# The order in which an instruction's waits are listed, in a gated mix of full and sliding-window attention

## The chip, the cores and the metric

The kernel runs on one core of one Trainium2 chip. The metric is the device time of one execution in microseconds (us). The median of three runs of the kernel before is 833.99 us, the lowest 832.91 and the highest 834.21.

## What is computed

Two attention blocks read the same input `x` (2048 tokens, width 640, 32 heads of 20) and are mixed by a gate per token.

```python
def _A_ref(x, wqkv, wo):                 # full attention
    q, k, v = qkv[0], qkv[1], qkv[2]
    scores = jnp.einsum("bhqd,bhkd->bhqk", q, k) * scale
    p = _softmax(scores, axis=-1)
    o = jnp.einsum("bhqk,bhkd->bhqd", p, v)
    return o.transpose(...).reshape(B, S, D) @ wo
def _B_ref(x, wqkv, wo):                 # 8 keys, each 2 apart, looking back
    idx = pos[:, None] - (jnp.arange(8) * 2)[None, :]
    logits = jnp.einsum("bhsd,bhswd->bhsw", q, kg) * scale
    attn = _softmax(jnp.where(mask, logits, -1e9), axis=-1)
    ...
g = _sigmoid((x * gate_w).sum(-1, keepdims=True))
return g * a + (1 - g) * b
```

## The kernel before

**Full attention.** The work is cut into 32 groups: 4 blocks of 512 queries by 8 quads of heads (four heads lie on the four 32-row strips of TensorE). A group has 64 units, one for each of 16 key blocks and 4 heads: a matmul of keys by queries into one PSUM bank of 512 columns. Two or three units make a tile. For each tile s, `qk(s)` (L1524) writes the scores to `score[s % 2]`, and `exp(s)` (L1547) on ACT turns them into `ebuf[s % 5]`. `pv` (L1592) multiplies the exps by the values and accumulates them in `obank`. So tile s+2 can't be scored before exp(s) has read its buffer, and exp(s) writes a buffer that exp(s-5) wrote and that pv has read since.

Some units take another way ("rides"): a third matmul of `qk` goes into a side bank, and DVE makes an exponential out of it by integer arithmetic on bf16 bits (L1537 into `uD`, L806 with shifted copies into `eD`), for which GpSimd scales the values (L798 into `vS`).

**Everything else** is fitted in between: projections, the gate, the sliding attention B (L841 to L1000), the normalisation of each group (L767 to L781) and the output projection. Their matmuls go through `mm_group` (L566) into three side banks, two of which are the third banks of the score buffers. L1613 is a filler matmul.

**What sets the order.** A planner, `_Sched`, is run while the program is built. `task()` lays out each operation on one of five streams (SP for DMA issues, ACT, PE, DVE, POOL), finds the earlier tasks that it must wait for (`deps`: for each stream the youngest task alone, its own included, and each DMA for itself), and estimates its `end` from given durations and from the delay `LAT` of each stream (0.22 us for PE, 0.18 ACT, 0.13 DVE, 0.15 POOL, 0.1 SP). `idx` is a task's number in the order of layout. `next_tile`, `step`, `spend` and the generators use these estimates to choose what is laid out next.

`emit()` then writes each stream out in its order. For each task it goes through the task's `deps` and calls `wait_ge` for each semaphore value that this stream hasn't waited for yet; then it issues the operation. In the built program an instruction holds one wait: the first wait listed for a task stays on its (first) instruction, and each further one becomes an instruction of its own ahead of it, EVENT_SEMAPHORE in the profile, all of them from L285. For an exp of the kernel before, the list is the wait for exp(s-5) on ACT's own semaphore and then the wait for `qk(s)` on PE's. The first sits on the exp; the second is the separate instruction ahead of it. A DMA's wait for its own semaphore's earlier use follows after these.

By engine, the built program of before has this many instructions with two or more waits, and separate wait instructions in all:

| | instructions | with several waits | separate waits |
|---|---|---|---|
| ACT | 764 | 742 | 751 |
| PE | 12389 | 423 | 447 |
| DVE | 1191 | 164 | 166 |
| POOL | 194 | 25 | 29 |
| SP | 723 | 118 | 131 |

Of the kernel before, what the change touches and what calls it, by code (L numbers as in the profile page):

```python
# [115 lines left out]
LAT = {"pe": 0.22, "act": 0.18, "dve": 0.13, "pool": 0.15, "sp": 0.1}  # L116
# [20 lines left out]
class _Sched:  # L137
# [107 lines left out]
    def emit(self):  # L245
        for sname in self.STREAMS:
            ccount = 0
            pool = self.dma_sems.get(sname)
            rot = 0
            totals = {}  # L250
            for t in self.lists[sname]:
                if not t.mark:
                    continue
                if t.dom == "cmp":
                    ccount += 1
                    t.sem = self.sems[sname]
                    t.val = ccount
                else:
                    sem = pool[rot % len(pool)]
                    rot += 1  # L260
                    prev = totals.get(sem, 0)
                    t.sem = sem
                    t.prev_total = prev
                    t.val = prev + 16 * t.nd
                    totals[sem] = t.val
            for sem, tot in totals.items():
                self.dma_final[sem] = tot
        nc = self.nc
        names = {"sp": "sync", "act": "scalar", "pe": "tensor", "dve": "vector", "pool": "gpsimd"}
        with nc.allow_low_precision(reason="bf16 kernel"), nc.allow_non_contiguous_dma(  # L270
            reason="small layout loads"
        ), nc.Block() as blk:
            for sname in self.STREAMS:
                lst = self.lists[sname]
                if not lst:
                    continue

                def body(eng, lst=lst, sname=sname):
                    waited = {}
                    for t in lst:  # L280
                        for d in sorted(t.deps, key=lambda x: x.idx):
                            if d.val is None:
                                raise RuntimeError("unmarked dep")
                            if d.val > waited.get(d.sem, 0):
                                eng.wait_ge(d.sem, d.val)  # L285
                                waited[d.sem] = d.val
                        if t.dom == "dma" and t.prev_total > waited.get(t.sem, 0):
                            eng.wait_ge(t.sem, t.prev_total)
                            waited[t.sem] = t.prev_total
                        ins = t.fn(eng)  # L290
                        if t.mark:
                            group = ins if isinstance(ins, list) else [ins]
                            assert len(group) == t.nd and group[0] is not None
                            for i_ in group:
                                i_.then_inc(t.sem, 16 if t.dom == "dma" else 1)
                    if sname == "sp":
                        for sem, tot in self.dma_final.items():
                            if tot > waited.get(sem, 0):
                                eng.wait_ge(sem, tot)

                getattr(blk, names[sname])(body)
# [1485 lines left out]
```

## Time and profile before

| | |
|---|---|
| median of the runs | 833.99 us (832.91 to 834.21) |
| span of the profiled execution, first to last instruction | 830.2 us |
| granted TensorE clock over the span | 0.999 |
| first and last start of an exp (L1547) | 19.1 and 818.3 us |
| HBM read, written | 11.94 MB, 2.62 MB |
| DMA queue of the loads and copies, share of 16 engines | 12.5% |

The profile is of one execution. Its span leaves out what lies before the first and after the last of the program's own instructions, 3.8 us against the median of the runs. Busy times on PE come from modelled ends of pipelined matmuls; on ACT and DVE one instruction's record overlaps the next one's, so the pace is read from starts. Semaphore instructions aren't counted as busy. A wait is credited to the engine that met it last.

### The profile page before, as it was taken

What the parts mean: (1) busy time and instruction counts of PE and PEld (TensorE: products, weight loads), DVE (VectorE), ACT (ScalarE), POOL (GpSimd) and SP (SyncE); (2) the same over time, 40 slices, a digit from 0 to 9 for tenths busy, and PEclk for the clock granted to TensorE, in tenths of its full rate; (3) what the DMA queues carried; (4) which work ended last, traced back from release to release, by engine and by line L of the source; (5) the groups of instructions that cost most, each with busy time, mean ns of one, the idle gap of its engine ahead of it and who ended that gap; (6) DMA issues with size and microseconds to landing.
All of it is one profiled execution on the core that took longest, in us unless ns stands there. A gap on an engine that the chain in (4) does not pass through costs nothing.

```text
span 830.2 us, 29189 instructions
## 1 busy us (share of the span) xinstructions
PE 776.4 (94%) x12389; PEld 284.4 (34%) x12389; DVE 679.5 (82%) x1191; ACT 802.8 (97%) x763; POOL 139.1 (17%) x194
## 2 busy tenths in 40 slices
PE   8999999998999899999999998899999999998898
PEld 5332232333333332333244233333333433343223
DVE  7667787789989878887898988898887977889973
ACT  4999999999999999999999999999999999999995
POOL 5022111620211111021201011111011111101110
PEclk9999999999999999999999999999999999999999
DMA  9112210200111010011001011100111011100001
GB/s 310 35 36 47 47 35 19 71 21 15 36 34 31 24 29 20 7 40 34 18 18 44 19 20 41 31 22 7 34 30 27 6 39 33 33 7 21 21 6 34
DMA packets 45014, 29.12 MB, mean 35 GB/s; under 512 B 27204, under 2 KB 43684, under 8 KB 44884
## 3 DMA queue, kind: packets, MB, share of 16 engines
q1 hardware_dynamic: 44596, 26.92, 12.5%
q8 instruction: 98, 1.61, 0.8%
q10 hardware_dynamic: 288, 0.33, 0.1%
q14 instruction: 32, 0.26, 0.1%
HBM read 11.94 MB, written 2.62 MB: 18 GB/s over the span
## 4 chain that ended last, share of the span: by engine, by line
ACT 49%; PE 34%; issue 13%; DVE 4%; DVEq 0%; ACTq 0%
ACT ebuf L1547 49%; PE score L1524 10%; PE obank L1592 8%; PE side L566 8%; PE score L566 4%; DVE uD L1537 1%; DVE eD L806 1%; PE obank L468 1%; PE score L1239 1%; PE obank L1613 1%; ACT eB L923 0%; PE side L1262 0%; PE score L1613 0%; ACT tB L957 0%; PE score L693 0%
## 5 line engine op out<-in xcount | busy, mean ns | idle before, releaser
L1547 ACT ACTIVATE ebuf<-score 128x1024 bf16<-128x1024 f32 (+1 forms) x731 | 791.4, 1232 | 8.8 <-PE score L1524 6.7
L1524 PE MATMUL score<-qT,kT 32*128 32x512 bf16 x2048 | 290.9, 383 | 35.9 <-ACT ebuf L1547 24.3
L1537 DVE TENSOR_SCALAR uD<-score 128x512 int16<-128x512 f32 x324 | 217.1, 684 | 41.6 <-PE score L1524 38.9
L806 DVE TENSOR_SCALAR eD<-uD 128x2048 int16<-128x2048 int16 x243 | 169.0, 725 | 5.8 <-PE obank L1592 5.2
L1524 PEld LDWEIGHTS score<-qT,kT 32*128 32x128 bf16 x2048 | 74.9, 91 | 281.7 <-ACT ebuf L1547 121.0
L1592 PE MATMUL obank<-ebuf,vA 128*21 128x512 bf16 x1724 | 160.3, 385 | 2.6 <-ACT ebuf L1547 1.9
L798 POOL TENSOR_TENSOR vS<-vA,vw 128x252 bf16<-128x252 bf16 x81 | 60.2, 744 | 317.0 <-PE obank L1592 283.7
L566 PE MATMUL side<-xT,kvw 128*32 128x256 bf16 (+1 forms) x2540 | 102.6, 280 | 2.1 <-DVE qkvB L862 1.0
L1592 PE MATMUL obank<-eD,vS 128*21 128x512 bf16 x972 | 83.4, 379 | 0.3 <-DVE eD L806 0.3
L566 PEld LDWEIGHTS side<-xT,kvw 128*32 128x32 bf16 x2540 | 59.6, 96 | 34.8 <-issue 19.0
L1592 PEld LDWEIGHTS obank<-ebuf,vA 128*21 128x21 bf16 x1724 | 38.0, 89 | 87.7 <-issue 74.6
L773 POOL TENSOR_TENSOR rcp<-rcp,gA 128x16 f32<-128x16 f32 x31 | 8.7, 282 | 280.2 <-DVE rcp L771 280.2
L979 DVE TENSOR_TENSOR stage<-qkvB,repB 128x1280 bf16<-128x1280 bf16 x64 | 52.9, 852 | 0.0
L878 DVE TENSOR_TENSOR stage<-qkvB 128x1280 bf16<-128x1280 bf16 x64 | 52.6, 850 | 0.2
L862 DVE CAST qkvB<-side 128x512 bf16<-128x512 f32 (+1 forms) x72 | 42.0, 593 | 9.3 <-PE side L566 9.0
L566 PE MATMUL side<-stage,ident 128*32 128x512 bf16 (+1 forms) x736 | 47.9, 349 | 1.7 <-DVE oB L996 0.9
L779 POOL TENSOR_TENSOR oN<-oTt,rcp 128x512 bf16<-128x512 f32 x31 | 32.9, 1062 | 2.4
L767 DVE STREAM_TRANSPOSE oTt<-obank 128x512 f32<-128x512 f32 x32 | 22.8, 712 | 11.2 <-PE obank L1592 10.7
L1592 PE MATMUL obank<-uD,vA 128*21 128x512 bf16 x324 | 31.5, 379 | 0.0
L1592 PEld LDWEIGHTS obank<-eD,vS 128*21 128x21 bf16 x972 | 23.5, 91 | 16.2 <-issue 2.5
L1613 PE MATMUL obank<-xT,zero 128*32 128x512 bf16 x296 | 26.6, 384 | 0.0
L566 PE MATMUL side<-woA_d,oTd 128*32 128x512 bf16 (+2 forms) x520 | 26.0, 295 | 0.0
(169 smaller groups left out, 542.0 us busy)
## 6 DMA issues: line engine op xcount, KB each, us to landing
repB<-eB SPq DMA_DIRECT2D x128, 32.0 KB
WqP<-in_A_wqkv_dram SPq DMA_DIRECT2D x16, 160.0 KB
stage<-in_B_wqkv_dram SPq DMA_DIRECT2D x1, 2400.0 KB
oTd<-oN SPq DMA_DIRECT2D x108, 20.0 KB
qT<-dst SPq DMA_DIRECT2D x104, 20.0 KB
out_dram<-outsb SPq DMA_DIRECT2D x12, 160.0 KB
kvw<-in_A_wqkv_dram SPq DMA_DIRECT2D x2, 800.0 KB
oTd<-in_A_x_dram SPq DMA_DIRECT2D x2, 640.0 KB
```

The lines of the kernel that those rows point to most:

```text
L566: ins = e.matmul(o[j:k, :], l(j) if callable(l) else l[:, j:k], r, start=(first and i == 0), stop=(last and i == n - 1), skip_group_check= ...
L779: T(en, c2, lambda e: e.tensor_tensor(oo, ii, ib, ALU.mult), reads=["rcp", "oTt"], writes=["oN0"])
L798: T("pool", 0.7, lambda e: e.tensor_tensor(vS[:, d % 2, :, :], _ap(vA, (kb * NQ + q) * 4 * DV, [[0, K - 1], [1, 4 * DV]]), _ap(vw, 0, [[1, ...
L806: T("dve", 0.11 + 0.1334 * n, lambda e, k=k, sl=sl: e.tensor_scalar(eD[:, sl % NS, 0:512 * n].bitcast(I16), uD[d % 2][:, 0:512 * n].bitcas ...
L862: t = TB(dvc(n * TOK), lambda e, o=o, i=i: e.tensor_copy(o, i), reads=[("side", b)], writes=[key])
L878: TB(dvc(CN * TOK, 2), lambda e, w=w, ks=ks: e.tensor_tensor(prodB(w), qB[:, :, :], ks, ALU.mult), reads=["qB", "kB"], writes=[("prod", w) ...
L979: TB(dvc(CN * TOK, 2), lambda e, w=w, vs=vs, rr=rr: e.tensor_tensor(prodB(w), vs, rr, ALU.mult), reads=["vB", ("repB", w4 % NR)], writes=[ ...
L1524: ins = e.matmul(o, kT[32 * j:32 * j + 32, q, kb * P:(kb + 1) * P], qT[g % NQT][32 * j:32 * j + 32, :], start=True, stop=True)
L1537: t = T("dve", 0.69, lambda e: e.tensor_scalar(uD[d % 2][:, 512 * i:512 * (i + 1)].bitcast(I16), side[x], UOFF, 0.0, op0=ALU.add, op1=ALU. ...
L1547: exps[s] = T("act", actc(512 * n), lambda e: e.activation(ebuf[s % NE][:, 0:512 * n], score[s % 2][:, 0:512 * n], ACTF.Exp, scale=LN2 / S ...
L1592: ins = e.matmul(obank[32 * j:32 * j + DV, :], v, src, start=(kb == 0), stop=(last and k >= len(lst) - 4), skip_group_check=True)
L1613: ins = e.matmul(o[32 * j:32 * j + 32, :], w[:, 32 * j:32 * j + 32] if best else w[:, :], xT[:, 0, 0:512], start=bool(best), stop=bool(bes ...
```

## The change

The waits of a task are sorted by the time at which the planner expects each to be met, `end` plus the delay of its stream, the latest first. Before, they were sorted by `idx`, the oldest in the layout first.

```diff
                     for t in lst:
-                        for d in sorted(t.deps, key=lambda x: x.idx):
+                        for d in sorted(t.deps, key=lambda x: -x.end - LAT[x.stream]):
                             if d.val is None:
                                 raise RuntimeError("unmarked dep")
                             if d.val > waited.get(d.sem, 0):
```

The plan itself, what runs on which engine and in which order, isn't touched. The sorted list decides which wait sits on the instruction and which ones stand apart, ahead of it. For an exp the list becomes `qk(s)` on PE's semaphore and then exp(s-5), so the wait for the scores sits on the exp. Where a stream waits twice for one semaphore, the larger value may now come first and make the smaller one unnecessary: PE has 446 separate waits after, and the other engines' numbers are the same.

## Prediction

> **What bounds the kernel now.** I read the page first: the busy line, the chain, the largest groups.
>
> ```profile
> span 830.2 us, 29189 instructions
> PE 776.4 (94%) x12389; PEld 284.4 (34%) x12389; DVE 679.5 (82%) x1191; ACT 802.8 (97%) x763; POOL 139.1 (17%) x194
> ...
> ACT 49%; PE 34%; issue 13%; DVE 4%; DVEq 0%; ACTq 0%
> ...
> L1547 ACT ACTIVATE ebuf<-score 128x1024 bf16<-128x1024 f32 (+1 forms) x731 | 791.4, 1232 | 8.8 <-PE score L1524 6.7
> ```
>
> ACT and PE share the bound, and 13% of the chain is "issue", in which nothing the profile names was running. The 8.8 us of idle time before the exps is too kind: consecutive ACT records overlap. By their start times, an exp of 1024 columns follows another after 904 ns at best and one of 1536 after 1330 ns. 469 of the one and 262 of the other make 469 x 0.904 + 262 x 1.330 = 772 us. The exps run from 19.1 to 819.3 us, so some 28 us in this stretch are not exp at full pace. In 144 places the next start came straight off a wait; these lost 18.4 us against that spacing.
>
> Next, the waits view, and the view of line 285, where every separate wait instruction comes from.
>
> ```profile
> PEld score L1524 <- ACT ebuf L1547: 121.0, 288, 1.2
> ...
> DVE uD L1537 <- PE score L1524: 38.9, 72, 2.0
> ```
>
> ```profile
> L285 ACTq EVENT_SEMAPHORE  x749: 17/17/38, 10.5 to 826.1; - x188
> L285 PEldq EVENT_SEMAPHORE  x445: 51/51/1052, 4.0 to 823.1; - x149
> L285 DVEq EVENT_SEMAPHORE  x164: 21/21/907, 17.7 to 825.3; - x164
> L285 POOLq EVENT_SEMAPHORE  x25: 17/17/17, 4.3 to 784.4; - x25
> ```
>
> PE and ACT hand work back and forth; almost every exp, and 445 places on PE, pass through a separate wait. Such a record takes 17 to 51 ns, but what a handover costs is not its length. So I took, for each instruction that waits, the time at which its last semaphore reached the awaited count (the trace's semaphore records, joined with each engine's waits in program order) and its start. Where the engine was free, the delays fall into two sharp groups:
>
> ```
> last wait met is on:     the instruction itself   a separate wait ahead of it
> ACT  release to start          22 ns                   82 ns
> DVE  release to start          23 ns                   92 ns
> POOL release to start          67 ns                  132 ns
> PE   to weight load            41 ns                  104 ns
> PE   to first matmul           45 ns                  135 ns
> PE   to end of 3-matmul scores 461 ns                 548 ns
> ```
>
> The timeline shows the last kind directly:
>
> ```profile
> 740.46 0.10 PEld L1524 LDWEIGHTS score<-qT,kT 32*128 32x128 bf16 x3 [0.21 <-ACT ebuf L1547]
> 740.46 0.39 PE L1524 MATMUL score<-qT,kT 32*128 32x512 bf16 x3
> ...
> 741.24 0.13 PEld L1524 LDWEIGHTS score<-qT,kT 32*128 32x128 bf16 x3 [0.36 <-issue]
> 741.27 0.39 PE L1524 MATMUL score<-qT,kT 32*128 32x512 bf16 x3 [0.20 <-ACT ebuf L1547]
> ```
>
> The first group has one wait, and load and matmul start together; the second has two, and the matmul starts 0.03 us behind its load, as if the instructions behind the separate wait were fetched only once it had ended.
>
> **The change, part by part.** It adds and removes no work: every engine has the same instructions in the same order, and the number of separate waits stays (751 on ACT, 166 on DVE, 29 on POOL, 131 on SP; 447 becomes 446 on PE). What moves is which wait sits on the instruction: it differs in 742 instructions of ACT, 331 of PE, 160 of DVE, 24 of POOL and 47 DMA issues of SP. The first wait listed stays on the instruction. By layout that is the oldest task: for an exp, its own engine's exp five tiles back, met microseconds ago, so the wait for the scores, which ends last, stands apart. The new list puts the scores' wait on the exp.
>
> Price of one handover, from the rows above: ACT 82 - 22 = 60 ns; PE 548 - 461 = 87 ns; DVE 92 - 23 = 69 ns, say 70; POOL 65 ns.
>
> How many are on the path? I followed the trace back from the last instruction: to the releaser where a start lay at one of the delays above, else to the instruction before it on its engine. (The page's chain can't be used for this count: a separate wait may end while ACT still runs the exp before, and the chain hops to PE all the same.) The path has 221 handovers and no DMA. Last met on a separate wait before and on the instruction after, by the release times of this trace: 74 on ACT, 49 on PE, 18 on DVE. Nine more on PE keep their late wait apart, 71 have it on the instruction in both.
>
> Sum along this path: 74 x 0.060 + 49 x 0.087 + 18 x 0.070 = 4.4 + 4.3 + 1.3 = 10.0 us. More than that can't go as long as durations stay, since this path remains.
>
> It may be less, for another path may take over. The lower reading cuts each handover to what its engine stood still beyond its usual spacing (904 or 1330 ns on ACT; 205 to 315 ns on PE by the pair of lines): 3.5 on ACT, 3.5 on PE, 1.3 on DVE, together 8.3 us. The paths that take over have separate waits too, so they shorten as well; but some run long on ACT alone. I take 8.3, and 10.0 as the far end.
>
> What is taken at nothing:
> - A separate wait that is met early. On PE, a score group behind an out-projection group starts after 312 ns with or without one; 162 of 215 exps whose scores had been ready over 320 ns start at full pace to 5 ns. Their number stays, so if this cover failed it would cost the same before and after.
> - Waits that the new order puts wrongly: by this trace 7 on PE and 2 on POOL go from the instruction to a separate wait, but only two of them bind: 2 x 0.087 = 0.2 us if both came onto the path; they are not on it now.
> - SP's 47 DMA issues. No row prices them; by the other engines' rows each may come 0 to 70 ns earlier. Nothing on the path waits for a DMA, so 0.
> - POOL, 22 such handovers at 65 ns, with 691 us idle and none on the path: 0.
>
> The stall removed goes to the other waits of the same loop: PE's single waits for ACT (148 starts, 35 us of excess spacing) are on the instruction already and don't shrink.
>
> 830.2 - 8.3 = 821.9 us of span. The runs' median is 834.0, 3.8 us over the span; with this kept, 825.7.
>
> [...]
>
> **The rivals.**
> 1. *The gain is taken back by another bound.* If PE's and DVE's part only lengthens waits elsewhere, ACT's handovers cut to lost spacing remain: 3.5 us, 830.5 us. For it: PE is 94% busy and ACT 97%; 23 of the 74 ACT handovers have less than 50 ns of lost spacing. Against: ACT lost 18.4 us behind PE and PE 78 us in excess spacing, both far more than the gain.
> 2. *The delay belongs to having several waits, not to which one is last.* Then 834.0. Against: of PE's starts with several waits, those 12 whose last one was on the instruction and bound came at 41 ns like single ones. For: it is only these few, and none on ACT.
> 3. *Slower: DVE and GpSimd collide more.* Starts move by up to 10 us, and the 243 shifted-copy operations of DVE take 906 ns on average where GpSimd is at work beside them (45 of them) and 684 ns elsewhere.
>
> ```profile
> L806 DVE TENSOR_SCALAR eD<-uD x243: 629/686/1798, 49.3 to 807.7; 128x2048 int16<-128x2048 int16 x122
> ```
>
> Each new collision costs 0.22 us if the path waits for it. 38 more eat the 8.3 us; 90 in place of 45 would give 825.7 + 10.0 = 835.7, if all were on the path. For it: the spread to 1798 ns. Against: GpSimd is busy 17% and follows the same order; this line has 12.3 us of the path in all, at some 0.7 us each 17 of the 243.
>
> **How the numbers follow.** The forecast, a gain of 5 to 11 us, has 0.82; rival 1, 0.11; rival 2, 0.04; rival 3, 0.03. Time 825.7. The range runs from 823.0 (the 10.0 us, with 1 us for the runs' own spread of 832.9 to 834.2) to 829.5 (half of PE's and DVE's part lost as in rival 1, 834.0 - 3.5 - 2.4 = 828.1, and the same spread). A measurement of this kernel can tell about 0.2%, 1.7 us, from no change: faster is the forecast and nearly all of rival 1, 0.93; same 0.04; slower 0.03.
>
> **What would show it.** In the profile after: exps bound by the scores start 22 ns behind the release; score matmuls start with their weight load, not 0.03 us behind; PE's groups end 461 ns behind the release; ACT's 18.4 us of lost spacing shrink to 9 to 12; the share of "issue" in the chain falls. The prediction is wrong if the delays move as said and the span doesn't (rival 1), if delays with late waits attached stay at 82 and 104 (rival 2), or if the 906 ns class of line 806 grows (rival 3).

## The result, and the profile after

| | kernel before | kernel after |
|---|---|---|
| median of the first five runs each | 833.99 us | 827.38 us (827.07 to 827.95) |
| ratio, 95% interval | | 0.9928 [0.9916, 0.9940] |
| measured again, other executions of before | 831.83 us median of 15 (831.70 to 834.04) | 827.94 us (827.01 to 829.45), ratio 0.9949 [0.9936, 0.9962] |
| span of the profiled execution | 830.2 us | 826.0 us |

The kernel is faster, by some 0.5 to 0.7%. The two ratios differ because the kernel before varies from one execution to the next, between 831.7 and 834.3 us; its first five runs happened to lie high. By these ratios the gain is 4.2 to 6.0 us; from profile to profile it is 4.2 us.

The page after, the same lines:

```profile
span 826.0 us, 29186 instructions
PE 775.0 (94%) x12387; PEld 281.2 (34%) x12389; DVE 679.2 (82%) x1191; ACT 800.2 (97%) x763; POOL 140.7 (17%) x194
...
ACT 52%; PE 25%; issue 20%; DVE 3%; ACTq 0%; DVEq 0%
...
L1547 ACT ACTIVATE ebuf<-score 128x1024 bf16<-128x1024 f32 (+1 forms) x731 | 789.3, 1275 | 6.7 <-PE score L1524 5.7
```

The busy times are those of before (two matmul records fewer were kept and one separate wait is less, no work is gone). "issue" has grown from 13 to 20%, though waits became shorter; the prediction had it fall. The share says little of the time: in a run shown below, which leaves out nearly all separate waits of ACT and has the same span of 826.0 us, it is 0%:

```profile
ACT 75%; PE 22%; DVE 2%; issue 0%; DVEq 0%
```

The chain goes by whichever wait the profile ties to an instruction, and the change moves just these. The line to look at is the exp's: its mean record grew from 1232 to 1275 ns, with the same shapes. That is the subject of most of what follows.

The waits view, the view of line 285 and the shifted copies:

```profile
PEld score L1524 <- ACT ebuf L1547: 202.9, 483, 1.2
...
DVE uD L1537 <- PE score L1524: 38.4, 69, 2.1
```

```profile
L285 ACTq EVENT_SEMAPHORE  x749: 17/17/38, 10.0 to 821.9; - x188
L285 PEldq EVENT_SEMAPHORE  x444: 51/51/842, 4.0 to 819.0; - x148
L285 DVEq EVENT_SEMAPHORE  x164: 21/21/564, 16.8 to 819.0; - x164
L285 POOLq EVENT_SEMAPHORE  x25: 17/17/17, 4.3 to 776.3; - x25
```

```profile
L806 DVE TENSOR_SCALAR eD<-uD x243: 628/683/1805, 49.6 to 803.7; 128x2048 int16<-128x2048 int16 x122
```

As many separate waits as before, as short as before: their records alone don't show the change. The 121.0 us that PE's loads waited for ACT became 202.9, but 88.0 us of "issue" at the same place became 45.6, and the idle time before these loads is 281.7 us in one page and 282.0 in the other: again a matter of who is named. DVE's shifted copies are unchanged.

In the timeline, the group that stood for the slow handover before:

```profile
737.52 0.10 PEld L1524 LDWEIGHTS score<-qT,kT 32*128 32x128 bf16 x3 [0.30 <-ACT ebuf L1547]
737.52 0.39 PE L1524 MATMUL score<-qT,kT 32*128 32x512 bf16 x3
...
738.50 0.13 PEld L1524 LDWEIGHTS score<-qT,kT 32*128 32x128 bf16 x3 [0.54 <-DVE uD L1537]
738.53 0.39 PE L1524 MATMUL score<-qT,kT 32*128 32x512 bf16 x3
```

At 737.52 load and matmul now start together. At 738.50 they don't: this is a group whose last wait still stands apart. The delays from release to start, taken as in the prediction, are ACT 22 ns (113 starts), DVE 23, POOL 68, PE 41 to the load, 45 to the matmul and 461 to the end of the group; on the 32 starts of PE that still wait apart 104, 135 and 548.

### The profile page after: what moved, and what is told of

It is laid out like the page before. It is cut to its first block, busy times and chain, and to the rows that moved or that the text cites. A ratio compares the mean times of both kernels' runs of the same rounds, so it can differ in the third digit from the quotient of the medians.

```text
span 826.0 us, 29186 instructions
## 1 busy us (share of the span) xinstructions
PE 775.0 (94%) x12387; PEld 281.2 (34%) x12389; DVE 679.2 (82%) x1191; ACT 800.2 (97%) x763; POOL 140.7 (17%) x194
## 4 chain that ended last, share of the span: by engine, by line
ACT 52%; PE 25%; issue 20%; DVE 3%; ACTq 0%; DVEq 0%
ACT ebuf L1547 51%; PE score L1524 8%; PE obank L1592 5%; PE side L566 5%; PE score L566 4%; DVE uD L1537 1%; PE score L1239 1%; PE obank L468 1%; DVE eD L806 1%; ACT eB L923 0%; PE obank L1613 0%; PE side L1262 0%; ACT tB L957 0%; PE score L1613 0%; ACTq L285 0%
## 5 line engine op out<-in xcount | busy, mean ns | idle before, releaser
L1547 ACT ACTIVATE ebuf<-score 128x1024 bf16<-128x1024 f32 (+1 forms) x731 | 789.3, 1275 | 6.7 <-PE score L1524 5.7
L1524 PEld LDWEIGHTS score<-qT,kT 32*128 32x128 bf16 x2048 | 71.6, 91 | 282.0 <-ACT ebuf L1547 202.9
L798 POOL TENSOR_TENSOR vS<-vA,vw 128x252 bf16<-128x252 bf16 x81 | 62.0, 767 | 313.2 <-PE obank L1592 279.6
L767 DVE STREAM_TRANSPOSE oTt<-obank 128x512 f32<-128x512 f32 x32 | 22.8, 711 | 11.4 <-PE obank L1592 10.8
L1592 PEld LDWEIGHTS obank<-eD,vS 128*21 128x21 bf16 x972 | 23.5, 91 | 16.1 <-DVE eD L806 1.4
```

Source lines behind the costliest of these rows:

```text
L798: T("pool", 0.7, lambda e: e.tensor_tensor(vS[:, d % 2, :, :], _ap(vA, (kb * NQ + q) * 4 * DV, [[0, K - 1], [1, 4 * DV]]), _ap(vw, 0, [[1, ...
L1524: ins = e.matmul(o, kT[32 * j:32 * j + 32, q, kb * P:(kb + 1) * P], qT[g % NQT][32 * j:32 * j + 32, :], start=True, stop=True)
L1547: exps[s] = T("act", actc(512 * n), lambda e: e.activation(ebuf[s % NE][:, 0:512 * n], score[s % 2][:, 0:512 * n], ACTF.Exp, scale=LN2 / S ...
L1592: ins = e.matmul(obank[32 * j:32 * j + DV, :], v, src, start=(kb == 0), stop=(last and k >= len(lst) - 4), skip_group_check=True)
```

## The experiments

All ratios are to the kernel before on the same chip; its median over 27 executions was 832.54 us beside the first four runs, 832.58 over 15 beside the next three, 831.83 over 15 beside the last four.

**The kernel before, unchanged.**

> The kernel before, unchanged, for the spans of several of its executions. The change took 6.6 us off the median but 4.2 us off the profiled span (830.2 to 826.0). If the profiled execution of before was a fast one, its spans lie around 832.0 to 832.4 (the median less the 1.8 us that the kernel after has around its span). If the change shortens what lies around the span, they lie around 830.2.

Measured: 832.61 us, ratio 0.9999 [0.9991, 1.0008]. In each of the 11 executions the time is 1.8 us above the span, as in the kernel after, while the spans go from 829.9 to 832.2. So nothing around the span changed, and the profiled execution of before (830.2) was one of the shorter ones. The first median of before, 833.99, came from long ones.

**One engine's lists at a time.** Three kernels sort the waits latest first on ACT alone, on PE alone, and on DVE, POOL and SP alone.

```diff
-                        for d in sorted(t.deps, key=lambda x: x.idx):
+                        for d in sorted(t.deps, key=lambda x: -x.end - LAT[x.stream] if sname in ('act',) else x.idx):
```

> Latest first on ACT alone, layout order elsewhere. By the price of handovers: ACT's release-to-start falls from 82 to 22 ns, PE's and DVE's stay at 104 and 92; 74 x 0.060 = 4.4 us at most, 3.5 us with each cut to its lost spacing, and 0.8 of that (as in the whole change, 6.6 of 8.3) 2.8 us: 831.2 us. If the delay belongs to having several waits, 834.0. If only ACT's side matters (PE's and DVE's part is lost elsewhere), all of the 6.6 us: 827.4.

> Latest first on PE alone. By the price of handovers: 49 x 0.087 = 4.3 us at most, 3.5 cut, 2.8 scaled: 831.2 us; ACT's 82 ns stay. If PE's part is lost elsewhere: 834.0.

> Latest first on DVE, POOL and SP alone. By the price of handovers: DVE 18 x 0.070 = 1.3 us, scaled 1.0: 833.0 us, nothing from POOL and SP. If it is lost elsewhere: 834.0. If starts that move on DVE collide more with GpSimd: above 834.0.

| latest first on | us | ratio | by ratio, of 832.5 us | term in the prediction |
|---|---|---|---|---|
| ACT | 829.75 | 0.9967 [0.9955, 0.9980] | 2.7 us | 3.5 |
| PE | 831.24 | 0.9986 [0.9977, 0.9995] | 1.2 us | 3.5 |
| DVE, POOL, SP | 832.20 | 0.9994 [0.9984, 1.0003] | 0.5 us | 1.3 |

By the intervals the gains are 1.7 to 3.7, 0.4 to 1.9 and -0.2 to 1.3 us. The delays moved only where they should: with ACT alone, ACT's release-to-start is 22 ns and PE's loads stay at 104. ACT's part is what was expected; PE's is far less than its term; the rest can't be told from nothing. The exp's row in the run with ACT alone and then in the run with PE alone:

```profile
L1547 ACT ACTIVATE ebuf<-score 128x1024 bf16<-128x1024 f32 (+1 forms) x731 | 789.9, 1254 | 7.6 <-PE score L1524 6.4
```

```profile
L1547 ACT ACTIVATE ebuf<-score 128x1024 bf16<-128x1024 f32 (+1 forms) x731 | 791.0, 1243 | 7.8 <-PE score L1524 6.4
```

The mean record lies between the 1232 ns of before and the 1275 of after, the higher the more was gained: 1243 with PE, 1254 with ACT.

**All but ACT**, to see whether the parts add up (the same edit, with `x.idx` for `act` alone).

> Latest first on PE, DVE, POOL and SP, layout order on ACT. If the parts add up, PE's 1.2 and the rest's 0.5: 0.998 of before, 830.8 us. If PE's and DVE's earlier starts are worth more beside a slow ACT handover than alone, they reach the 2.2 that the whole change has over ACT alone: 830.3 us.

Measured: 830.72 us, 0.9979 [0.9970, 0.9988]. Its 0.21% and the 0.33% of ACT alone make 0.54%, between the 0.51% and 0.72% measured of the whole. Within the intervals the parts add, and no part is seen to need the other.

**Implied waits left out.** An exp's wait for the exp five tiles back is implied by its wait for the scores, whose own wait for a newer exp comes first. The first kernel leaves out such waits on ACT, the second on every stream:

```diff
...
+        for t in sorted((t for l in self.lists.values() for t in l), key=lambda x: x.idx):
+            have = known[t.stream]
+            keep[t.idx] = kept = []
+            for d in sorted(t.deps, key=lambda x: -x.end - LAT[x.stream]):
+                if t.stream in ('act',) and d.val <= have.get(d.sem, 0):
+                    continue
+                kept.append(d)
+                for sem, val in list(d.knows.items()) + [(d.sem, d.val)]:
+                    have[sem] = max(have.get(sem, 0), val)
...
+            t.knows = dict(have)
+        needed = lambda t: keep[t.idx]
...
-                        for d in sorted(t.deps, key=lambda x: x.idx):
+                        for d in sorted(needed(t), key=lambda x: -x.end - LAT[x.stream]):
```

> The kernel after, and on ACT no wait that is already implied by another one (an exp's wait for the exp five tiles back is implied by its wait for the scores): 751 separate waits on ACT become 3. If a separate wait that is met early costs nothing, as the prediction took it, the time of the kernel after: 827.4 us. If each costs its 17 ns record, 731 x 0.017 = 12 us less at most, 815; if only the 45 or so exps that start 17 ns late lose it, 0.8 us: 826.6.

> The kernel after, and no implied wait on any stream: separate waits 751 to 3 on ACT, 446 to 406 on PE, 166 to 84 on DVE, 29 to 5 on POOL. If early separate waits cost nothing, what is left is the late ones on PE that stand apart in the kernel after (13 on its path, 13 x 0.087 = 1.1 us at most), of which few are implied: 826.6 to 827.6 us. If separate waits cost by their number, clearly below e5.

Measured: 827.82 us, 0.9939 [0.9925, 0.9953], with ACT's implied waits gone; 827.87 us, 0.9943 [0.9930, 0.9956], with all of them gone. The page of the first begins

```profile
span 826.0 us, 28440 instructions
```

746 records fewer than after (748 separate waits of ACT are gone; two more matmul records were kept), and the same span. A separate wait that is met early costs nothing that can be measured here: 827.82 us without them, 827.38 and 827.94 with them. The 17 ns by which some exps start late are not theirs: 68 starts of 1024 columns still lie 917 to 922 ns apart in place of 904, against 65 in the kernel after.

**The latest wait apart, everywhere** (`key=lambda x: x.end + LAT[x.stream]`).

> The earliest wait first everywhere, so that the one expected last stands apart. By the price of handovers: the 12 bound starts of PE with several waits that had the late one on the instruction lose it too; on the path of before some 5 of them, 5 x 0.087 = 0.4 us: 834.0 to 834.8 us, the kernel before within 0.8 us. If the order of layout was otherwise a good one for the waits that tie: up to 836.

Measured: 832.02 us, 0.9996 [0.9987, 1.0005]. The time can't be told from that of before, so the order by layout was already about the worst one: on ACT, 146 exps bound by their scores start 82 ns behind the release, against 140 before.

**PE's remaining late waits listed first.** `LATE` holds the counts of ACT's and DVE's semaphores for which these groups wait.

```diff
-                        for d in sorted(t.deps, key=lambda x: -x.end - LAT[x.stream]):
+                        for d in sorted(t.deps, key=lambda x: -1e9 if sname == "pe" and x.dom == "cmp" and x.val in LATE.get(x.stream, ()) else -x.end - LAT[x.stream]):
```

> The kernel after, and the PE groups whose last wait still stood apart in its trace (61 for ACT, 5 for DVE) list that wait first. 13 of them are on its path: 13 x 0.087 = 1.1 us at most; if PE's earlier starts are mostly given back, as in the run that changed PE alone (1.2 to 1.8 of 4.3 us), 0.3 to 0.5 us: 827.0 to 827.3, hard to tell from the kernel after.

> The kernel after, unchanged, on the same chip as the others of this call, since the kernel before spreads from 831.7 to 834.3 us between executions: 827.4 us by its first five times, and 5.0 us below the median of before (832.55) of the larger sample, a ratio of 0.994.

Measured: 827.52 us, 0.9940 [0.9928, 0.9953], against 827.94 us, 0.9949 [0.9936, 0.9962], for the kernel after beside it. The edit did what it should: 2 starts of PE bound by a separate late wait are left of 32. The 0.4 us have the expected size, but lie inside both intervals. No version tried here is clearly faster than the kernel after.

**ACT's pace by itself.** The exp records that grow suggested that a start is recorded ahead of what ACT can really do. This kernel lets ACT run 128 exps that wait for no other engine:

```diff
     run_until(("norm", NG - 1))
+    for i in range(128):
+        T("act", actc(1024), lambda e, i=i: e.activation(
+            ebuf[i % NE][:, 0:1024], score[i % 2][:, 0:1024], ACTF.Exp, scale=LN2 / STEP),
+          reads=[("score", i % 2)], writes=[("ebuf", i % NE)])
     tail()
```

> The kernel after with 128 more exps of 1024 columns on ACT ahead of the last stage, each from score buffers that are ready, with no other engine at work; their results are not used. It measures ACT's pace by itself. If an exp takes 916 ns and only its recorded start runs ahead (ends 916 ns apart while starts are 904 apart, until the lead is used up), the ends lie 916 ns apart here too and the time grows by 128 x 0.916 = 117 us, with starts turning from 904 to 916 apart once the records are some 250 ns longer. If the 12 ns are contention with the work of other engines, ends and starts lie 904 apart: 115.7 us more, records staying at 1017 to 1024 ns.

Measured: 940.8 us, the span 939.0. The added exps fill a wait of ACT that was there anyway, so the total doesn't decide; their records do. The view of their line (minimum, median and longest record, first and last start) and the timeline of the end:

```profile
L1757 ACT ACTIVATE ebuf<-score x128: 1018/1852/2698, 815.2 to 930.0; 128x1024 bf16<-128x1024 f32 x128
```

```profile
929.97 2.70 ACT L1757 ACTIVATE ebuf<-score 128x1024 bf16<-128x1024 f32 x1
932.72 0.56 PEld L1072 LDWEIGHTS score<-outsb,oN 128*32 128x32 bf16 x24 [112.91 <-ACT ebuf L1757]
932.72 2.32 PE L1072 MATMUL score<-outsb,oN 128*32 128x128 bf16 x32 [112.61 <-ACT ebuf L1757]
```

One form of instruction, 1018 ns in the first record and 2698 in the last. From the third to the last, starts are 903.3 ns apart and ends 916.7. PE, which waits for the last exp, starts at 932.72, 0.05 us behind its end at 932.67, and ACT's semaphore counts each exp 9 or 10 ns behind its recorded end: the ends are real, and the starts run ahead of them by 13 ns an exp, through the whole run. Contention with another compute engine is out: the last work of PE ended at 820.1 us, DVE's before it, and the spacings are the same to the end. The expectation's detail that the starts would turn to 916 ns was wrong; they never did.

## Why the prediction came out as it did

The time (827.4 against 825.7) lies in the range of 823.0 to 829.5, and the delays moved as forecast. The gain did not: 8.3 us were forecast, and 4.2 to 6.0 came. That the time lies well inside the range is in part luck, as the point on the span shows.

- *Which wait sits on the instruction decides the handover.* Right, to the ns: 82 to 22 on ACT, 92 to 23 on DVE, 548 to 461 on PE. Rival 2 (several waits cost, whatever their order) falls: 111 of the 113 exps at 22 ns have two waits. That the instructions behind a separate wait are fetched only once it has ended was the author's reading of these delays; no trace shows it.
- *Taken at nothing:* early separate waits, confirmed by 748 of ACT's removed without effect (827.82 us, against 827.38 and 827.94 with them). POOL and SP cost nothing that shows in the kernel that changed them along with DVE: 832.20 us, a gain of -0.2 to 1.3 us for the three together.
- *Rival 3*, more collisions of DVE and GpSimd: line 806 has the same median and longest record, 686 and 1798 ns before, 683 and 1805 after. The class that was to grow didn't: counted by any overlap of records, 46 of the line's operations run beside GpSimd's in either trace, at 901 ns on average before and 907 after.
- *Two of the named signs* failed. The share of "issue" rose. ACT's 18.4 us of lost spacing, counted by starts, became 16.1 and not 9 to 12: 111 exps that follow another exp are bound by their scores after, against 140 before.
- *The span plus 3.8 us.* Wrong: 1.8 us lie around every span, before and after. The profile and the first median came from different executions. This hid part of the next error: a gain of 8.3 us was subtracted from a median 2 us above the profile's own execution. With 1.8 us the forecast would have been 823.7 and the range would have ended at 827.5, so that 827.4 lay at its very end and the 827.9 measured later outside. (The upper end is also 0.4 us above what its terms give: 828.1 and 1 us make 829.1.)
- *The sum.* 8.3 us of span were forecast and 4.2 came. In the runs with one engine, ACT's 3.5 became 2.7, PE's 3.5 became 1.2 and DVE's 1.3 became 0.5. Each alone came out smaller, but only PE's term lies clearly outside its interval (0.4 to 1.9).

Why the sum was too large is, for one part, in the step "469 x 0.904 + 262 x 1.330 = 772 us", which read ACT's pace from starts. The long run shows that ends are what counts: 916.7 ns for 1024 columns; for 1536, ends that follow each other without a stall lie 1343 ns apart in the trace of before. That makes 469 x 0.9167 + 262 x 1.343 = 782 us, so that of the 28 us that the prediction read as not at full pace, some 9 are ACT's own pace. It also changes what a stall costs. In an unbroken run of 1024 columns the recorded starts gain 13 ns with each exp; a stall shorter than this lead can delay a start and hardly an end: of the 74 ACT handovers on the path, 30 had delayed the end by less than 5 ns. And PE waits for ends: in the long run it started 0.05 us behind the last one. Cut by ends in place of starts, ACT's term is 2.4 us.

The rest was given back on the way from ACT to PE. Followed through the trace of after, the handovers of the old path became shorter by 3.0 us on ACT, 1.3 on DVE, and 2.0 on PE (1.7 of it behind ACT, where 11 of 40 score groups are now bound by PE's own order and not by their wait). On the same path the exps end later after their starts, by 3.2 us in sum: earlier starts without earlier ends. Other steps make -1.0. Together -3.0 - 1.3 - 2.0 + 3.2 - 1.0 = -4.1, the span's difference but for rounding.

In the run with PE alone, the same path tells where PE's part went. The handovers to PE are 2.3 us shorter and PE's own stretches 0.8. But 0.7 us come back in ACT's handovers, where ACT is still at the exp before when the scores are ready, and 0.9 in exps that end later after their starts. Other steps make -0.3, in all -1.8, the difference of the two spans.

ACT's records by themselves tell the same. The time by which the end of an exp lies further behind the end before than ACT's pace (916.4 and 1343 ns, the means where no stall lies between, in the trace of before) adds up as follows:

```
                  lost between exps' ends     span
before                 13.1 us               830.2
ACT alone              10.3                  827.8
PE alone               11.6                  828.4
DVE, POOL, SP          12.6                  829.2
after                   8.7                  826.0
```

What is no longer lost there is what the span gains, within 0.5 us. The two must go together, since the first exp ends 20.2 to 21.1 us into the span and 10.8 to 10.9 us lie behind the last one in all five; so the table tells where the time went and not why. So rival 1 was half right, and its 3.5 us lie nearer to the span's gain of 4.2 than the forecast's 8.3: the gain shrank because an engine was nearer to its bound than the starts showed, and the engine was ACT. What stays open is how much of PE's part each of the causes took: that PE's order takes over in 11 of 40 places, ACT's in others, and that earlier starts bring no earlier ends is read from the traces, but no run separates them.

## What to carry to other kernels

Where the first wait listed is the one that stays on the instruction, list first the wait that is met last, so that only waits met long before stand apart: here a handover that binds became 60 to 90 ns shorter, and 748 separate waits on ACT that are met early cost nothing that showed (827.82 us without them, 827.38 and 827.94 with them). Price such a change by counting handovers on the path, then cut each by what it delays at its consumer: read an engine's pace from the ends of back-to-back records or from semaphore updates, since starts may run ahead (here by 13 ns with each exp of 1024 columns). Before a gain in spans is turned into a time, check from several executions what lies around the span.

## What the runs showed of the hardware

- ACT's pace can't be read from its records' starts. In an unbroken run of 1024-column exps starts were 903.3 and ends 916.7 ns apart, and the records grew from 1018 to 2698 ns. Stalls reset them: behind each of the 46 stalls of over 100 ns in the trace of before, the exp's record is back at 7 or 8 ns above the shortest of its size.
- A late wait on a separate instruction delays the start by about the same on each of four engines (60 ns on ACT, 63 to PE's load, 65 on POOL, 69 on DVE), and on PE 24 to 27 ns more until the group is through.
- 748 separate waits on ACT that are met early cost nothing measurable: 827.82 without them, 827.38 and 827.94 with them.
